# A group normalisation kernel: 24 of 32 tiles moved into a staggered loop, and GpSimd's share of the scaling moved to VectorE

## The chip, the cores and the metric

The kernel runs on one core of one Trainium2 chip. The time is device microseconds of that core. Two numbers are compared by the ratio of fast runs with its 95% interval, and "same" means within 2%.

## The reference

```python
def reference(x, g, b):            # x: bf16 (128, 1024, 32, 16), G = 32 groups
    xr = x.reshape(B, G, C // G, H, W)
    mu = xr.mean(axis=(2, 3, 4), keepdims=True)
    var = ((xr - mu) ** 2).mean(axis=(2, 3, 4), keepdims=True)
    xn = ((xr - mu) / jnp.sqrt(var + 1e-5)).reshape(B, C, H, W)
    return xn * g[None, :, None, None] + b[None, :, None, None]
```

Four images with 32 groups each fill 128 partitions, so there are 32 tiles of 128 x 16384 bf16, 4.19 MB each. A tile is loaded, summed, squared with the mean taken off, scaled channel by channel (32 channels of 512 elements) in place, and stored from the same buffer. There are six buffers.

## The kernel before

Per tile `i`: TensorE sums the tile into PSUM (`M`: 32 products with an identity matrix), VectorE reduces that to the mean (`R0`), ScalarE squares and sums the two halves (`Q`), then takes the root (`V`), and the 32 channels are scaled on three engines: 16 on VectorE, 13 on GpSimd (`A`), and the last 3 on ScalarE, between the two squares of the next tile (`finish`). `finish` also stores the tile and loads another into the buffer of an older one. SyncE issues these loads and stores in order. (PSUM is the memory in which the kernel keeps the sums of TensorE.)

```python
def Q(i):
    ...
    squares(st, F // 2, 0, st["negmean"][:], 1.0, s0[:])
    v0 = spool.tile([P, 1], F32, name="v0")
    finish(i - 1)                       # 3 channels on ScalarE, store i-1, load i+4
    ...                                 # v0 = s0 / n + eps, on GpSimd
    squares(st, F // 2, 1, st["negmean"][:], 1.0, s1[:])

def A(i):
    if not in_parts(i):
        for n in range(POOL_SHARE):                       # 13
            scale_on("pool", i, KC - LAST_SHARE - POOL_SHARE + n)
        for k in range(KC - LAST_SHARE - POOL_SHARE):     # 16
            scale_on("dve", i, k)
        ...

for i in range(NT):                     # 32 tiles, written out
    Q(i)
    if i + 1 < NT:
        M(i + 1)
        R0(i + 1)
    V(i)
    A(i)
```

## Time and profile before

| | before |
|---|---|
| time | 634.7 us |
| span of the profiled run | 631.9 us |
| DMA rate in the middle slices | 424 to 438 GB/s |
| ScalarE busy | 539 us (85%) |
| VectorE busy | 380 us (60%) |
| GpSimd busy | 347 us (55%) |

These are lines of the page of the kernel before. In all views PE is TensorE, PEld its weight load, DVE is VectorE, ACT is ScalarE, POOL is GpSimd and SPq is the queue of SyncE. The span is cut into 40 equal slices. A digit is the busy share of a slice in tenths (9 is 90% or more), and the last row is what the DMA engines moved.

```profile
ACT  4589999999999897877997779977989797797960
...
DMA  8999999999999999999999999999999999999996
GB/s 365 431 437 423 430 431 429 431 433 431 424 430 432 431 431 429 430 433 438 428 432 429 433 431 429 430 430 433 434 431 431 430 430 432 433 426 436 433 418 271
```

The DMA engines are full from the first slice to the last. The kernel moves 268.4 MB; at 430 GB/s that is 624 us. A tile costs them 8.39 MB / 430 GB/s = 19.5 us, in and out.

The next lines are the costliest groups of instructions of the kernel before: source line, engine, operation, tiles, shapes, count; then busy time in us and mean ns of one; then the idle time of the engine before them and what ended it.

```profile
L244 ACT ACTIVATE ja<-xt,negmean 128x8192 fp8e5<-128x8192 bf16 x60 | 426.7, 7112 | 52.1 <-DVE jd L189 52.0
...
L368 DVE TENSOR_SCALAR xt<-xt,scl,bia 128x512 bf16<-128x512 bf16 x536 | 352.6, 732 | 40.0 <-POOL bia L353 40.0
L368 POOL TENSOR_SCALAR xt<-xt,scl,bia 128x512 bf16<-128x512 bf16 x390 | 308.7, 806 | 3.4 <-POOL bia L353 0.3
```

ScalarE's two squares a tile are the largest compute cost. (The mean of a VectorE channel, 732 ns, counts overlap with its neighbours: 16 in a row take 11.14 us, 0.70 each.) ScalarE's work on one tile is in this timeline of the kernel before (start, us, what; in brackets the idle time before it and what ended it):

```profile
318.37 7.12 ACT L244 ACTIVATE ja<-xt,negmean 128x8192 fp8e5<-128x8192 bf16 x1 [1.43 <-DVE jd L189]
...
325.49 2.21 ACT L363 ACTIVATE xt<-xt,bia,scl 128x512 bf16<-128x512 bf16 x3
327.60 7.11 ACT L244 ACTIVATE ja<-xt,negmean 128x8192 fp8e5<-128x8192 bf16 x1
...
334.90 0.29 ACT L308 ACTIVATE rstd<-s,v 128x1 f32<-128x1 f32 x1
338.27 7.12 ACT L244 ACTIVATE ja<-xt,negmean 128x8192 fp8e5<-128x8192 bf16 x1 [3.08 <-DVE jd L189]
```

From 318.37 to 335.2 it works 16.8 us without a gap, then it waits for the next tile's mean, which waits for that tile's load.

The last view of the kernel before is the issuing queue's own waits on SyncE (us in total, times, longest), and the transfers with their median time from issue to landing:

```profile
SPq L101 <- DMA out_dram<-xt: 425.4, 26, 19.0
SPq L381 <- DVE xt L368: 151.7, 18, 38.6
```

```profile
xt<-in_x_dram SPq DMA_DIRECT2D x30, 4096.0 KB, 29.3
out_dram<-xt SPq DMA_DIRECT2D x30, 4096.0 KB, 38.3
```

SyncE waits mostly before issuing a load, for an older store to free its buffer. A store needs some 9.75 us of DMA time (half of a tile's 19.5) but lands 38 us after issue, so I estimate that three other transfers are queued ahead of it. Compute is well ahead of the queue.

### The profile page before, as it was taken

The page shows a single profiled execution, that of the slowest core. Times are in us where ns is not written, and L with a number is a line of the kernel's source. Part 1 is how long each engine was busy: PE and PEld are TensorE (multiplying, and loading weights), DVE is VectorE, ACT ScalarE, POOL GpSimd, SP SyncE. Part 2 cuts the span into 40 slices and gives each one's busy share as a digit, 9 for nine tenths or more (in the row PEclk, how much of TensorE's full clock was granted, in tenths as well). Part 3 has the DMA queues.
Part 4 walks back from the last instruction along what each step waited for, and adds up shares of the span by engine and source line. Part 5 has one row for each costly group of instructions (what it writes and reads, how often), then busy time and mean ns, then how long its engine had stood idle before and what let it go on. Part 6 is the DMA issues. An engine that isn't in the chain of part 4 may idle for free.

```text
span 631.9 us, 3907 instructions
## 1 busy us (share of the span) xinstructions
PE 293.1 (46%) x1025; PEld 114.4 (18%) x1025; DVE 380.2 (60%) x645; ACT 539.0 (85%) x268; POOL 346.8 (55%) x523
## 2 busy tenths in 40 slices
PE   5578604553245633456433565335553345647000
PEld 2233201221112211122111222112221112213000
DVE  1087666666676576545775457754657654577660
ACT  4589999999999897877997779977989797797960
POOL 0077666666666576544775446764557654477100
PEclk9689758766787657876678766677865788658655
DMA  8999999999999999999999999999999999999996
GB/s 365 431 437 423 430 431 429 431 433 431 424 430 432 431 431 429 430 433 438 428 432 429 433 431 429 430 430 433 434 431 431 430 430 432 433 426 436 433 418 271
DMA packets 11063, 268.70 MB, mean 425 GB/s; under 512 B 1312, under 2 KB 1312, under 8 KB 1312
## 3 DMA queue, kind: packets, MB, share of 16 engines
q1 hardware_dynamic: 10944, 268.44, 99.0%
q8 instruction: 8, 0.13, 0.1%
q14 instruction: 15, 0.12, 0.0%
q10 hardware_dynamic: 96, 0.00, 0.0%
HBM read 134.22 MB, written 134.22 MB: 425 GB/s over the span
## 4 chain that ended last, share of the span: by engine, by line
DMA 67%; ACT 15%; PE 7%; issue 4%; DVE 3%; POOL 0%; SPq 0%; DVEq 0%; ACTq 0%; POOLq 0%
DMA out_dram<-xt 42%; DMA xt<-in_x_dram 25%; ACT ja L244 13%; PE pa L166 7%; DVE xt L368 3%; ACT xt L363 2%; DMA gb_b<-in_g_dram 1%; POOL scl L337 0%; SPq L101 0%; ACT rstd L308 0%; DVE rstd L312 0%; DVE jd L189 0%; POOL shift L343 0%; DVEq L455 0%; DVE bia L324 0%
## 5 line engine op out<-in xcount | busy, mean ns | idle before, releaser
L244 ACT ACTIVATE ja<-xt,negmean 128x8192 fp8e5<-128x8192 bf16 x60 | 426.7, 7112 | 52.1 <-DVE jd L189 52.0
L166 PE MATMUL pa<-xt,eye 128*128 128x512 bf16 x976 | 281.8, 460 | 289.7 <-DMA xt<-in_x_dram 278.5
L368 DVE TENSOR_SCALAR xt<-xt,scl,bia 128x512 bf16<-128x512 bf16 x536 | 352.6, 732 | 40.0 <-POOL bia L353 40.0
L368 POOL TENSOR_SCALAR xt<-xt,scl,bia 128x512 bf16<-128x512 bf16 x390 | 308.7, 806 | 3.4 <-POOL bia L353 0.3
L166 PEld LDWEIGHTS <-eye 128*128 128x128 bf16 x1024 | 114.3, 114 | 468.5 <-DMA xt<-in_x_dram 290.6
L337 POOL TENSOR_SCALAR scl<-gb,rstd 128x32 f32<-128x32 f32 x31 | 11.2, 361 | 218.2 <-DVE rstd L312 218.2
L189 DVE TENSOR_SCALAR_CACHE_REDUCE jd<-pa 128x512 bf16<-128x512 f32 x32 | 22.0, 688 | 149.0 <-PE pa L166 149.0
L363 ACT ACTIVATE xt<-xt,bia,scl 128x512 bf16<-128x512 bf16 x98 | 72.0, 798 | 0.8 <-DVE bia L324 0.8
L244 ACT ACTIVATE ja<-xt,q 128x4096 fp8e5<-128x4096 bf16 x8 | 29.6, 3706 | 6.6 <-DVE jd L189 6.4
L312 DVE RECIPROCAL rstd<-rstd 128x1 f32<-128x1 f32 x32 | 5.1, 160 | 35.8 <-ACT rstd L308 35.8
L343 POOL TENSOR_SCALAR shift<-scl,negmean 128x32 f32<-128x32 f32 x31 | 11.2, 360 | 3.1
L216 POOL TENSOR_SCALAR off<-negmean,q 128x1 f32<-128x1 f32 x2 | 0.9, 432 | 20.5 <-DVE jd L189 20.5
L166 PE MATMUL pb<-xt,eye 128*128 128x512 bf16 x48 | 11.6, 388 | 1.0 <-DMA xt<-in_x_dram 1.0
L308 ACT ACTIVATE rstd<-s,v 128x1 f32<-128x1 f32 x30 | 8.8, 294 | 2.8
L244 ACT ACTIVATION_READ_ACCUMULATOR ja<-xt,negmean 128x1 f32 x60 | 11.2, 187 | 0.0
L353 POOL TENSOR_TENSOR bia<-shift,gb 128x32 f32<-128x32 f32 x31 | 7.8, 252 | 2.6
L308 ACT ACTIVATE rstd<-var,eps_t 128x1 f32<-128x1 f32 x2 | 0.6, 295 | 9.2 <-DVE jv L292 9.2
L273 POOL TENSOR_SCALAR v<-s 128x1 f32<-128x1 f32 x30 | 5.8, 192 | 2.5
L156 DVE COPY gb<-gb_p 128x64 f32<-128x64 f32 x1 | 0.2, 224 | 5.6 <-PE gb_p L148 5.6
L116 ACT ACT_TABLE_LOAD x1 | 1.3, 1283 | 1.7 <-PEq L444 1.7
L189 DVE DVE_READ_ACCUMULATOR jd<-pa 128x1 f32 x32 | 2.6, 81 | 0.0
L292 DVE TENSOR_SCALAR_CACHE_REDUCE jv<-sq,seed 128x4 f32<-128x4 f32 x2 | 0.4, 216 | 2.7 <-ACT ja L244 2.7
(18 smaller groups left out, 6.1 us busy)
## 6 DMA issues: line engine op xcount, KB each, us to landing
xt<-in_x_dram SPq DMA_DIRECT2D x30, 4096.0 KB, 29.3
out_dram<-xt SPq DMA_DIRECT2D x30, 4096.0 KB, 38.3
xt<-in_x_dram SPq DMA_DIRECT2D x8, 1024.0 KB, 16.5
out_dram<-xt SPq DMA_DIRECT2D x8, 1024.0 KB, 17.8
gb_b<-in_g_dram ACTq DMA_DIRECT2D x1, 2.0 KB, 3.2
gb_b<-in_b_dram ACTq DMA_DIRECT2D x1, 2.0 KB, 5.3
```

The source lines that it names most:

```text
L116: chain("act", nc.scalar.activation(out=warm[:], in_=eps_t[:], func=ACT.Sqrt))
L166: nc.tensor.matmul(out=ps[:], lhsT=eye[:], rhs=st["xt"][:, k * MMN : (k + 1) * MMN], start=(k == lo), stop=(k == hi - 1),),
L189: nc.vector.tensor_scalar(out=jd[:], in0=ps[:], scalar1=-inv_n, scalar2=seed, op0=ALU.mult, op1=ALU.add, accum_out=total[:],),
L244: nc.scalar.activation(out=ja[:, 0:w], in_=st["xt"][:, k * w : (k + 1) * w], func=ACT.Square, bias=bias, scale=scale, accum_out=sq, satura ...
L273: nc.gpsimd.tensor_scalar(out=v0[:], in0=s0[:], scalar1=inv_n, scalar2=EPS, op0=ALU.mult, op1=ALU.add,),
L308: nc.scalar.activation(out=rstd[:], in_=last_sum[:], func=ACT.Sqrt, bias=bias[:], scale=scale),
L312: chain("dve", nc.vector.reciprocal(out=rstd[:], in_=rstd[:]))
L337: nc.gpsimd.tensor_scalar(out=scl[:], in0=gam, scalar1=rstd[:], scalar2=None, op0=ALU.mult),
L343: nc.gpsimd.tensor_scalar(out=shift[:], in0=scl[:], scalar1=st["negmean"][:], scalar2=None, op0=ALU.mult,),
L353: nc.gpsimd.tensor_tensor(out=bia[:], in0=shift[:], in1=bet, op=ALU.add),
L363: inst = nc.scalar.activation(out=span, in_=span, func=ACT.Identity, bias=bia, scale=scl)
L368: inst = eng.tensor_scalar(out=span, in0=span, scalar1=scl, scalar2=bia, op0=ALU.mult, op1=ALU.add,)
```

## The change

The intent, as I read it: tiles 2 to 25 run in a loop of four trips of six tiles. One call of `tick` works on one tile, so a trip, one pass through the loop's body, is six ticks. The loop's head is aligned in memory for all engines (`head_align_engines`), I take it for the sake of instruction fetch. TensorE sums only half of a tile, and VectorE adds the two quarters of the other half in one instruction with an accumulator (`R`). GpSimd's 13 channels go to VectorE, which scales 29. The loop is "staggered": its body is cut into four stages, and the semaphores of a stage are reset while another runs. For that no engine may enter a stage before every engine has signalled that it is done with the stage two before. By default an engine gives this signal at the end of the stage in between, so a boundary is in effect a meeting of all five engines' instruction streams.

```diff
+    def M(s):
+        matmuls(s, banks[s], 0, NMM // 2)
+
+    def R(s):
+        t = small[s]
+        chain("dve", nc.vector.scalar_tensor_tensor(
+                out=jd[:], in0=xts[s][:, HF : HF + QF], scalar=1.0,
+                in1=xts[s][:, HF + QF : F], op0=ALU.mult, op1=ALU.add,
+                accum_out=t["half"][:], saturate=False))
+        sum_of(banks[s], 1.0, t["half"][:], t["total"][:])
+        ...
+    def A(s):
+        for k in range(KC - ACT_SHARE):          # 29
+            scale_on("dve", s, k)
+
+    def tick(i, s, load, cut):
+        before, after, free = (s - 1) % SLOTS, (s + 1) % SLOTS, (s - 2) % SLOTS
+        Q0(s)                                    # first square
+        finish(i - 1, before)                    # 3 channels on ScalarE, store i-1
+        if cut:
+            tc.stage_boundary()
+        if load:
+            L(i - 2 + SLOTS, free)
+        Q1(s)                                    # second square, root
+        M(after)
+        R(after)
+        V(s)
+        A(s)
 ...
+    with tc.For_i(
+        0, TRIPS * SLOTS, SLOTS, iteration_sync="staggered", hint_engines=(), head_align_engines=ENGINES
+    ) as iv:
+        for c in range(SLOTS):
+            tick(iv + FIRST + c, (FIRST + c) % SLOTS, True, c == 1 or c == 4)
+            if c == 2:
+                tc.stage_boundary()
+    last.clear()
+    tc.epilogue_barrier()
 ...
```

Two of the four boundaries lie behind `finish` in the middle of a tick (`c` = 1 and 4), two at the end of a tick (`c` = 2 and the loop's end). Also changed: the first load comes in halves, not quarters, the last load whole, and the last two stores in halves.

## The prediction

> **What bounds the kernel now.** The DMA engines. The table of 40 slices shows them at 90% or more in all slices but the first and last, at 424 to 438 GB/s; 268.4 MB at the usual 430 GB/s is 624 us of a 631.9 us span. In 4 us windows, data moves from about 2 us to 626 us without a gap. The Trainium skill (DMA: Bandwidth & Descriptors, Specifications) gives 435 GB/s as the fabric's ceiling; the trace agrees, at 430. So a tile (4.19 MB in, 4.19 MB out) takes 19.5 us. The other engines need less per tile: ScalarE two squares of 7.3 us, three channels (2.2 us) and a root, 17.1 us; VectorE 12 us (16 channels of 0.70 us, a 0.69 us sum); GpSimd 11.3 us; TensorE 9 to 10 us. The queue's own waits confirm it: before issuing loads it waits 425 us for earlier stores, so compute is ahead. A store takes 38 us to land and a load 29 us, four and three tiles' worth of one-way traffic: the queue is always deep.
>
> **What the change does, per tile.** GpSimd loses its 13 channels. VectorE takes 29, each at 0.33 us rather than 0.70 (the tile scaled without GpSimd near the end: 16 in 5.26 us), so 9.6 us; the skill (SBUF — State Buffer, Who interferes with whom) explains it: both engines share a port pair under an exclusive lock. VectorE also adds half of the tile: 4096 pairs, by the slope of the 0.69 us sum of 512 an estimated 4.3 us. VectorE: about 15 us, still under 19.5. TensorE sums 16 pieces, not 32: about 4.6 us, beside VectorE's half, so the mean comes some 4 us earlier. ScalarE is unchanged at 17.1 us. None of this is on the critical path, which is DMA.
>
> **What the loop adds.** Four stage boundaries a trip, at which engines wait for each other, and four trips. ScalarE now runs one to two tiles ahead of the DMA queue; the boundaries take some of this lead. I estimate delays up to 20 us for ScalarE at a boundary, and stores up to 10 us later, against 19.5 us or more of queued traffic: the DMA engines should not run dry inside the loop. Where they may: entering the loop (waiting for all six loads, landing at about 64 us, and the first store, at about 74 us, delays the second store: 0 to 4 us lost) and leaving it (a barrier that waits for the last loads and stores empties the queue; then a square of 7.3 us and three channels stand before the next store: 0 to 14 us). The end gains little: the last stores are queued behind older ones until 626 us, so a mean 4 us earlier is hidden. Fewer instructions save nothing visible: instruction fetches are 0.25 MB.
>
> **Prediction.** 635.5 us, 8 in 10 between 628 and 650. Faster by over 2% would need under 622 us, below the DMA time at 430 GB/s: 3%. Within 2%: 80%. Slower: 17%.
>
> **What would show it.** Right: 427 to 433 GB/s in all middle slices; VectorE channels at 0.33 us; GpSimd busy under 10%; TensorE about half; ScalarE still about 540 us. The two doubtful slices are at 60 to 80 us and near 520 us: a dip of GB/s there is the loop's entry or exit.
>
> **What would make it wrong.** An exit barrier that drains everything, or boundaries that stall the queue's issuing by more than 19.5 us every trip, would give 650 us or more. The half-tile add much above 4.3 us (over 9) would make VectorE the bound. A DMA rate that rises by a per cent[...], would give 628.

## More of the kernel before

A run is quoted as the median of its executions. The runs were taken on several chips; the kernel before was run again beside each, and its medians lie between 634.1 and 634.7 us.

## The result, and the profile after

| | before | after |
|---|---|---|
| time | 634.65 us (634.36 to 634.85, 4 runs) | 660.13 us (659.54 to 660.86, 4 runs) |
| span of the profiled run | 631.9 us | 659.1 us |
| ScalarE busy | 539 us | 539 us |
| VectorE busy | 380 us | 470 us |
| GpSimd busy | 347 us | 46 us |
| TensorE busy | 293 us | 166 us |

The ratio is 1.0402 (1.0384 to 1.042). A ratio is the mean time of one kernel's fast runs over that of the other's of the same rounds, so it is not quite the ratio of the medians quoted. The change is 25.5 us slower.

The same lines of the page, after:

```profile
ACT  3884987789598959877895989598778959999993
...
DMA  9999999999999999999999999999999999998576
GB/s 382 420 439 407 436 426 434 418 422 426 420 426 402 418 443 394 412 437 418 404 434 414 418 412 430 430 386 412 443 416 404 426 422 407 380 443 386 255 319 286
```

Two things changed. The middle slices no longer sit at 430: they swing around 418. And the last four slices, about 65 us, drop to 255 to 386, while ScalarE, nearly done with its work before, is now busy to the end. The windows of the changed kernel put numbers on both: three trips of the loop, and the end (the columns are the stretch, its length, busy us and instructions of PE, PEld, DVE, ACT and POOL, granted clock of TensorE, DMA share, GB/s).

```profile
106.00:226.80 120.80, 29.80 (x94) 11.06 (x96) 89.55 (x211) 100.25 (x49) 8.77 (x24) 0.61 1.00 420
226.80:347.50 120.70, 28.99 (x94) 10.93 (x96) 89.46 (x211) 100.14 (x49) 8.77 (x24) 0.63 0.99 419
347.50:468.20 120.70, 29.91 (x94) 11.21 (x96) 89.45 (x211) 100.01 (x49) 8.52 (x24) 0.61 0.99 418
...
600.00:648.00 48.00, 4.11 (x20) 1.67 (x17) 36.24 (x105) 46.16 (x30) 3.35 (x10) 0.60 0.67 284
```

A trip takes 120.7 us, 20.1 us a tile against 19.5; 24 tiles times 0.62 us are 15 us. The other 10 us are lost behind the loop: the rate is 401 GB/s from 542 to 580 us, and from 600 us on the DMA engines are busy two thirds of the time. There the last load, issued at 570.60, has landed (a load takes 24 us), and only stores are left. ScalarE finishes a tile in 16.8 us, and one store of 4.19 MB in 16.8 us is only 250 GB/s (an estimate from these two numbers). So a pace that is enough while loads and stores share the DMA engines is not enough at the end, unless stores are already waiting in the queue.

The DMA share in the trips still reads 0.99 to 1.00. The share of busy time alone would say "DMA bound"; the GB/s and the queue's waits say otherwise. In the changed kernel SyncE no longer waits for old stores before loading; it waits before storing, for compute. And its stores land after 15 us, not 38: the queue is shallow.

```profile
SPq L134 <- DVE xt L334: 408.5, 26, 33.8
SPq L134 <- ACT xt L330: 77.9, 9, 18.5
...
SPq L125 <- DMA out_dram<-xt: 4.9, 1, 4.9
```

```profile
xt<-in_x_dram SPq DMA_DIRECT2D x31, 4096.0 KB, 24.4
out_dram<-xt SPq DMA_DIRECT2D x30, 4096.0 KB, 15.0
```

The chain of work that ended last was DMA for 67% before (first line) and is ScalarE for 57% after (second line):

```profile
DMA 67%; ACT 15%; PE 7%; issue 4%; DVE 3%; POOL 0%; SPq 0%; DVEq 0%; ACTq 0%; POOLq 0%
ACT 57%; issue 21%; DVE 9%; DMA 7%; PE 3%; POOL 1%; ACTq 0%; SPq 0%; DVEq 0%; POOLq 0%
```

The groups that answer to those of before show that the pieces themselves cost what was forecast. The half-tile add, new, takes 4.42 us.

```profile
L254 ACT ACTIVATE ja<-xt,negmean 128x8192 fp8e5<-128x8192 bf16 x60 | 426.7, 7111 | 91.6 <-DVE xt L334 55.5
L334 DVE TENSOR_SCALAR xt<-xt,scl,bia 128x512 bf16<-128x512 bf16 x926 | 302.2, 406 | 40.7 <-POOL bia L320 40.6
...
L228 DVE SCALAR_TENSOR_TENSOR jd<-xt 128x4096 fp8e5<-128x4096 bf16 x30 | 132.6, 4419 | 12.2 <-issue 7.3
```

ScalarE's squares are as long as before, but ScalarE idles 91.6 us before them. Where it does is in its timeline over three ticks, half a trip:

```profile
239.72 7.12 ACT L254 ACTIVATE ja<-xt,negmean 128x8192 fp8e5<-128x8192 bf16 x1 [7.38 <-DVE xt L334]
...
263.56 2.21 ACT L330 ACTIVATE xt<-xt,bia,scl 128x512 bf16<-128x512 bf16 x3
268.35 7.12 ACT L254 ACTIVATE ja<-xt,negmean 128x8192 fp8e5<-128x8192 bf16 x1 [2.58 <-issue]
...
292.38 0.29 ACT L285 ACTIVATE rstd<-s,v 128x1 f32<-128x1 f32 x1
300.13 7.12 ACT L254 ACTIVATE ja<-xt,negmean 128x8192 fp8e5<-128x8192 bf16 x1 [7.46 <-DVE xt L334]
```

From 239.72 to 300.13 are 60.4 us for three tiles: 50.4 us of work without gaps, and 2.58 us at the mid-tick boundary and 7.46 us at the end-of-tick boundary. Three tiles of DMA are 58.5 us. So in the loop ScalarE with its two waits is slower than the DMA engines, by 1.9 us per three tiles. Eight such pairs of waits, and 11.05 us once at the loop's entry, make up the 91.6 us.

Whom does it wait for? These are VectorE's channels and SyncE's issues of the same stretch:

```profile
258.03 9.47 DVE L334 TENSOR_SCALAR xt<-xt,scl,bia 128x512 bf16<-128x512 bf16 x29 [1.29 <-POOL bia L320]
...
294.15 9.46 DVE L334 TENSOR_SCALAR xt<-xt,scl,bia 128x512 bf16<-128x512 bf16 x29 [1.29 <-POOL bia L320]
```

```profile
267.70 0.34 SPq L134 DMA_DIRECT2D out_dram<-xt  x1
268.65 0.35 SPq L125 DMA_DIRECT2D xt<-in_x_dram  x1
```

At the end of a tick ScalarE has delivered the root at 292.67. VectorE scales its 29 channels from 294.15 to 303.6, and its signal stands behind them. ScalarE goes on at 300.13, some 3.5 us before the last channel ends: my reading, which no run tests, is that VectorE's instruction stream runs some ten short instructions ahead of its arithmetic (in e3 below the gap is 3.6 us, with 32 channels). At the mid-tick boundary the one who is late is SyncE: its store (267.70) waits for VectorE's channels (done at 267.5), and ScalarE goes on at 268.35. So ScalarE waits for VectorE, whose channels in turn waited for ScalarE's root. In the written-out kernel ScalarE starts the next square in this time.

### The profile page after: what moved, and what is told of

It reads as the page before. It is cut to its first block, busy times and chain, and to the rows that moved or that the text cites. A ratio compares the mean times of both kernels' runs of the same rounds, so it can differ in the third digit from the quotient of the medians.

```text
span 659.1 us, 3426 instructions
## 1 busy us (share of the span) xinstructions
PE 166.1 (25%) x535; PEld 62.7 (10%) x545; DVE 470.1 (71%) x1126; ACT 538.8 (82%) x268; POOL 45.7 (7%) x133
## 4 chain that ended last, share of the span: by engine, by line
ACT 57%; issue 21%; DVE 9%; DMA 7%; PE 3%; POOL 1%; ACTq 0%; SPq 0%; DVEq 0%; POOLq 0%
ACT ja L254 48%; DVE xt L334 8%; ACT xt L330 8%; DMA out_dram<-xt 4%; DMA xt<-in_x_dram 3%; PE ps L195 3%; ACT rstd L285 1%; POOL scl L300 0%; POOL shift L310 0%; POOL bia L320 0%; DVE jd L207 0%; DVE rstd L296 0%; SPq L125 0%; DVE sp_jv L398 0%; ACTq L450 0%
## 5 line engine op out<-in xcount | busy, mean ns | idle before, releaser
L254 ACT ACTIVATE ja<-xt,negmean 128x8192 fp8e5<-128x8192 bf16 x60 | 426.7, 7111 | 91.6 <-DVE xt L334 55.5
L334 DVE TENSOR_SCALAR xt<-xt,scl,bia 128x512 bf16<-128x512 bf16 x926 | 302.2, 406 | 40.7 <-POOL bia L320 40.6
L195 PE MATMUL ps<-xt,eye 128*128 128x512 bf16 x518 | 159.3, 476 | 414.8 <-issue 288.3
L228 DVE SCALAR_TENSOR_TENSOR jd<-xt 128x4096 fp8e5<-128x4096 bf16 x30 | 132.6, 4419 | 12.2 <-issue 7.3
L195 PEld LDWEIGHTS <-eye 128*128 128x128 bf16 x544 | 62.6, 118 | 540.5 <-issue 483.4
L207 DVE TENSOR_SCALAR_CACHE_REDUCE jd<-ps,half 128x512 fp8e5<-128x512 f32 x30 | 22.5, 751 | 14.9 <-PE ps L195 12.4
L254 ACT ACTIVATE ja<-xt,sp_q 128x4096 fp8e5<-128x4096 bf16 x8 | 29.7, 3708 | 2.8 <-DVE jd L207 2.5
L270 POOL TENSOR_SCALAR v<-s 128x1 f32<-128x1 f32 x30 | 13.1, 436 | 244.5 <-ACT ja L254 244.5
L195 PE MATMUL bank_a<-xt,eye 128*128 128x512 bf16 x16 | 7.1, 628 | 23.2 <-DMA xt<-in_x_dram 23.2
L207 DVE TENSOR_SCALAR_CACHE_REDUCE jd<-bank_a 128x512 fp8e5<-128x512 f32 x2 | 1.4, 686 | 6.6 <-PE bank_a L195 6.6
L242 DVE TENSOR_SCALAR negmean<-total 128x1 f32<-128x1 f32 x30 | 4.6, 154 | 1.0
```

Source lines behind the costliest of these rows:

```text
L195: nc.tensor.matmul(out=ps[:], lhsT=eye[:], rhs=xts[s][:, k * MMN : (k + 1) * MMN], start=(k == lo), stop=(k == hi - 1),),
L207: nc.vector.tensor_scalar(out=jd[:, 0:MMN], in0=ps[:], scalar1=factor, scalar2=seed, op0=ALU.mult, op1=ALU.add, accum_out=total, saturate= ...
L228: nc.vector.scalar_tensor_tensor(out=jd[:], in0=xts[s][:, HF : HF + QF], scalar=1.0, in1=xts[s][:, HF + QF : F], op0=ALU.mult, op1=ALU.add ...
L254: nc.scalar.activation(out=ja[:, 0:w], in_=xts[s][:, k * w : (k + 1) * w], func=ACT.Square, bias=bias, scale=scale, accum_out=sq, saturate ...
L270: nc.gpsimd.tensor_scalar(out=t["v0"][:], in0=t["s0"][:], scalar1=inv_n, scalar2=EPS, op0=ALU.mult, op1=ALU.add,),
L334: inst = nc.vector.tensor_scalar(out=span, in0=span, scalar1=scl, scalar2=bia, op0=ALU.mult, op1=ALU.add,)
```

## The experiments

The theory: the stage boundaries make ScalarE and VectorE take turns; 20 us of waits a trip exceed ScalarE's slack of 6 x 2.7 = 16 us a trip; and since ScalarE never gets ahead of the queue, the tiles behind the loop run at ScalarE's pace. The rivals: the new split (29 channels and the half-tile add on VectorE) is slower by itself; or the back edge (the jump from the end of the loop's body to its head) and instruction fetch cost the time; or the loop's entry and exit do.

All outputs are right.

| run | time, us | ratio to before (95%) |
|---|---|---|
| e1 loop written out | 636.9 | 1.0044 (1.0031 to 1.0058) |
| e2 VectorE signals early | 645.1 | 1.0175 (1.016 to 1.0191) |
| e3 no channels on ScalarE | 662.2 | 1.0443 (1.0427 to 1.0459) |
| e4 two trips | 642.6 | 1.0131 (1.0115 to 1.0146) |
| e5 e2 and two trips | 636.5 | 1.0031 (1.0016 to 1.0046) |
| e6 e1, no channels on ScalarE | 637.2 | 1.0047 (1.0032 to 1.0062) |
| e7 no half-tile add | 685.5 | 1.0811 (1.0795 to 1.0828) |
| e8 e1, last parts in quarters | 636.7 | 1.0045 (1.0031 to 1.0059) |
| e9 all engines signal early | 634.6 | 1.0001 (0.9986 to 1.0016) |
| e10 not aligned | 660.2 | 1.04 (1.0384 to 1.0416) |
| e11 e8, first load in quarters | 637.2 | 1.0046 (1.0032 to 1.006) |
| e12 before, GpSimd's channels to VectorE | 636.1 | 1.0027 (1.0014 to 1.0041) |
| e13 e9 with three trips | 634.0 | 0.999 (0.9977 to 1.0004) |
| e14 e9, one channel on ScalarE | 633.3 | 0.9978 (0.9965 to 0.9992) |

**e1: the loop written out.**

```diff
-    tc.prologue_barrier()
-    with tc.For_i(0, TRIPS * SLOTS, SLOTS, iteration_sync="staggered", ...) as iv:
-        for c in range(SLOTS):
-            tick(iv + FIRST + c, (FIRST + c) % SLOTS, True, c == 1 or c == 4)
-            if c == 2:
-                tc.stage_boundary()
-    tc.epilogue_barrier()
+    for i in range(FIRST, FIRST + TRIPS * SLOTS):
+        tick(i, i % SLOTS, True, False)
```

> The changed kernel with the loop written out: the same ticks in the same order, the same split of the work, no stage boundaries. Theory (boundaries): ScalarE works 16.8 us a tile and loses 10.0 us per three tiles at the boundaries, 60.4 us against 58.5 us of DMA; without boundaries it needs 50.4 us, DMA is the bound again, and the kernel takes 632 to 637 us, with ScalarE idle in no fixed pattern and stores landing 35 us or more after issue. Rival (the new split: 29 channels and the half-tile add on VectorE): the time stays above 652 us.

Measured: 636.9 us. The whole split of the work is kept, and 23 of the 25.5 us are gone, so the split by itself is not the cause. The queue is deep again; stores land 38 us after issue. The issuing queue's waits of this run are as before:

```profile
SPq L125 <- DMA out_dram<-xt: 462.3, 26, 19.5
SPq L134 <- DVE xt L333: 116.9, 11, 32.7
```

**e2: only VectorE's signal moved to an early place in each stage.**

```diff
         M(after)
         R(after)
+        if early:                       # ticks 0, 1, 3 and 4: once in each stage
+            tc.previous_stage_wait(mybir.EngineType.DVE)
         V(s)
         A(s)
```

> The changed kernel with its loop; only VectorE's signal that its previous stage is done stands early in each stage (after the mean of the next tile), not behind the 29 channels at the end of the stage. Theory: the 7.4 us that ScalarE idles at every other boundary is the wait for VectorE's sequencer to get through those channels; it falls to 2 us or less, the loop falls from 60.4 to 58.5 to 59 us per three tiles, and the kernel takes 635 to 645 us. Rivals (the back edge and its instruction fetch, or the new split): 657 to 662 us.

Measured: 645.13 us, just above the range. Nothing but the place of a signal was changed, and it is worth 15 us. ScalarE's timeline in this run shows the end-of-tick wait at 1.50 us rather than 7.46, with the mid-tick wait now 3.94 to 6.84 us (2.57 only at the first boundary):

```profile
286.12 7.12 ACT L256 ACTIVATE ja<-xt,negmean 128x8192 fp8e5<-128x8192 bf16 x1 [1.50 <-issue]
...
318.53 7.12 ACT L256 ACTIVATE ja<-xt,negmean 128x8192 fp8e5<-128x8192 bf16 x1 [3.94 <-issue]
```

From 227.33 to 286.12 to 344.27, three tiles take 58.8 and 58.2 us: the loop runs at the DMA's pace. What is left, 8 us against e1, lies at the end (columns as in the windows above):

```profile
560.00:580.00 20.00, 5.70 (x16) 2.08 (x17) 16.89 (x43) 19.92 (x9) 2.32 (x7) 0.67 0.99 415
580.00:600.00 20.00, 8.99 (x32) 3.47 (x31) 18.17 (x47) 19.91 (x9) 1.34 (x4) 0.76 0.86 369
600.00:612.00 12.00, 0.00 (x0) 0.00 (x0) 5.51 (x18) 11.79 (x9) 1.34 (x4) 0.50 0.62 265
```

ScalarE is busy all the time there, and from 580 us on the DMA engines are not: compute left the loop without a lead.

**e3: no channels on ScalarE, 32 on VectorE.** Edit: `ACT_SHARE = 3` becomes `0`, which holds for all tiles but the last two, inside the loop and outside.

> The changed kernel with no channels on ScalarE in the loop: VectorE takes all 32. Theory (ScalarE's work and the boundary idle add up): ScalarE per three tiles 44 us of work, idle 8.4 and some 5.7 us at the two boundaries, since VectorE's channels take 1 us longer, sum 58 us, so near the DMA's 58.5; the end is shorter too; 635 to 645 us. Rival (VectorE has too much work): slower than the changed kernel, above 662 us.

Measured: 662.2 us, where my theory said 635 to 645. This is a miss. I had treated the waits as sums with fixed parts. The mid-tick wait was as forecast (5.6 us), but the one at the end of a tick grew to 10.9 us, not 8.4:

```profile
302.43 7.12 ACT L254 ACTIVATE ja<-xt,negmean 128x8192 fp8e5<-128x8192 bf16 x1 [10.94 <-DVE xt L334]
...
329.96 7.12 ACT L254 ACTIVATE ja<-xt,negmean 128x8192 fp8e5<-128x8192 bf16 x1 [5.58 <-issue]
```

In that tick VectorE takes the reciprocal at 354.87, behind its own mean work for the next tile, although ScalarE had the root at 352.3. With less to do, ScalarE only waits longer; three tiles take 60.7 us, about as in the changed kernel. It is a chain of turns, not a sum on one engine. By its time alone this run fits the rival "VectorE has too much work" as well, so e6 was made.

**e4: two trips, twelve tiles written out behind them.** Edit: `TRIPS = 4` becomes `2`.

> Two trips of the loop rather than four; 12 tiles are written out behind it. Theory: each looped tile costs the DMA engines 0.6 us, and 12 are enough for 7 us; behind the loop ScalarE catches up at 17 us a tile against 19.5, so the end is bound by DMA as in the kernel before: 640 to 646 us. If the cost were at the loop's entry and exit rather than inside, it would stay at 657 to 662 us.

Measured: 642.6 us, as forecast. Half the looped tiles cost 5.7 us over e1. In the 36 us behind the loop the rate is 403 GB/s, which costs an estimated 2 us against 430; after that it is back at 421 to 441 GB/s in every slice but the last. Entry and exit, which are both still there, are not where most of the time goes.

**e5: e2 and e4 together.**

> VectorE's early signal and two trips together. Theory: with the early signal the loop runs at the DMA's pace (58.0 to 58.7 us per three tiles), and what was left of the loss, 8 us, came from ScalarE leaving the loop without a lead over the queue; twelve tiles written out behind the loop give the lead back, so the end is bound by DMA: 636 to 639.5 us, as the kernel with the loop written out (636.9). Rival (entering the loop or the new split costs the rest): 642 us or more.

Measured: 636.5 us, as e1, though entry and exit of the loop are still there. Its loop runs at the DMA's pace and its written-out tiles win the lead back; together these return everything that writing the loop out returns.

**e6: e1 with all 32 channels on VectorE.** Edit: e1 and `ACT_SHARE = 0`.

> All 32 channels on VectorE, and the loop written out. The looped kernel with this split took 662.2 us. Theory (there the boundaries make ScalarE and VectorE take turns; VectorE's load by itself, some 16.5 us a tile against 19.5 of DMA, is harmless): 635 to 639 us. Rival (VectorE with 32 channels is too slow whatever the loop): above 650 us.

Measured: 637.2 us. The split that took 662.2 us in the loop is harmless without it. This settles e3: at these loads VectorE matters only through the boundaries.

**e7: no half-tile add; TensorE sums all 32 pieces.**

```diff
-        matmuls(s, banks[s], 0, NMM // 2)
+        matmuls(s, banks[s], 0, NMM)
-        chain("dve", nc.vector.scalar_tensor_tensor(...))       # the half-tile add
-        sum_of(banks[s], 1.0, t["half"][:], t["total"][:])
+        sum_of(banks[s], 1.0, None, t["total"][:])
```

> The changed kernel with its loop, but TensorE sums all 32 pieces and VectorE adds no half. Theory (a chain through the boundaries: behind the mid-tick boundary ScalarE's second square, 7.3 us, used to hide the sum for the next tile; 32 products at the low clock and the reduction take about 11 us): some 3 to 4 us more per three tiles, so 680 to 695 us. Rival (the half-tile add on VectorE is what slows the change): below 650 us.

Measured: 685.5 us. The half-tile add is not the cause; in this loop it helps. Behind the mid-tick boundary a third wait appears, for the mean of the next tile. It is some 3.06 us in one half of a trip and 2.05 in the other:

```profile
289.80 7.12 ACT L241 ACTIVATE ja<-xt,negmean 128x8192 fp8e5<-128x8192 bf16 x1 [3.06 <-DVE negmean L229]
...
352.42 7.12 ACT L241 ACTIVATE ja<-xt,negmean 128x8192 fp8e5<-128x8192 bf16 x1 [2.05 <-DVE rstd L283]
```

That is a little less than the 3 to 4 us I had written. Three tiles take 63.65 us (250.43 to 314.08) and 62.6 us (314.08 to 376.69) in turn, against 60.4. From ScalarE's first tile in the loop to its first one behind it are 505.3 us, against 483.6 in the changed kernel: 22 of the 25 us added. The other 3 were lost before the loop, which ScalarE enters at 61.79 us and not at 58.69.

**e8 and e11: the written-out kernel with the last load and stores in quarters (e8), and the first load in quarters too (e11), as in the kernel before.** Edits: the last load gets four parts; the last two tiles are stored after every eight channels; in e11 `2 if i == 0` becomes `NQ if i == 0`.

> The loop written out, and the last load and the last two stores in quarters as in the kernel before, not in one piece and in halves. Written out in halves it was 0.44% slower than before. Theory: bytes end at the same time in both, and the rest is the coarser last stores (16 KB rather than 8 KB pieces, so one engine finishes late): 633.5 to 635 us. If the residue lies elsewhere: 636 to 637.5 us.

> The loop written out, the last load and stores in quarters, and the first load in quarters too, as before. It looks for the 0.4% that is left against the kernel before. If the coarse first load is the cause: 633.5 to 635 us; if not, 636 to 637.5 us.

Measured: 636.7 and 637.2 us. Both guesses at the last 0.4% were wrong: neither changes the time, so the size of the first and last transfers is not it.

**e9: all engines signal early.**

```diff
             L(i - 2 + SLOTS, free)
+        if early and not cut:
+            tc.previous_stage_wait(mybir.EngineType.SP)
         Q1(s)
         M(after)
         R(after)
+        if early:
+            for e in (DVE, PE, Activation, Pool):
+                tc.previous_stage_wait(e)
```

> Four trips, and every engine's signal early in the stage: VectorE, TensorE, ScalarE and GpSimd after the mean of the next tile, and in every other stage SyncE after its first load. With VectorE's alone it took 645.1 us, and ScalarE still idled 4 to 7 us at the boundary in the middle of a tick, at which SyncE comes late because its store waits for VectorE's channels and then the queue. Theory: that idle falls in the loop's stages, ScalarE keeps some lead over the queue at the exit: 636 to 643 us. If the other engines' signals don't matter: 644 to 646 us.

Measured: 634.6 us, ratio 1.0001. This is better than the 636 to 643 us of my theory, which is a miss in its size. The loop, the alignment, the split and the boundaries are all kept, and the whole 25.5 us are gone. The waits did not all shrink: the end-of-tick wait reads 6.2 to 6.3 us, the mid-tick one 1.9. But three tiles take 58.5 us, and ScalarE waits for SyncE, which waits for the DMA queue; it is slack now, not a turn. The first two lines are ScalarE's timeline, the last is SyncE's largest wait in total, which in the changed kernel was for VectorE's channels (408.5 us).

```profile
280.36 7.12 ACT L256 ACTIVATE ja<-xt,negmean 128x8192 fp8e5<-128x8192 bf16 x1 [6.30 <-DVE xt L336]
...
338.83 7.12 ACT L256 ACTIVATE ja<-xt,negmean 128x8192 fp8e5<-128x8192 bf16 x1 [6.19 <-DVE xt L336]
...
SPq L136 <- DMA out_dram<-xt: 237.8, 22, 18.1
```

The releaser is given as VectorE's channels, though VectorE signals before them; SyncE's next load, issued at 279.55 and 338.10, is what stands just before both starts. This run moves the signals of four more engines than e2 at once; which of them matters was not tried one by one.

**e10: without the alignment to a fetch block.** Edit: `head_align_engines=ENGINES` removed.

> The changed kernel without the alignment of the loop to a fetch block. Theory: at the back edge ScalarE idles 7.4 us, as at the boundary in the middle of the body, so in the aligned kernel fetching costs nothing that shows; unaligned it may cost a few us at three back edges: 658 to 680 us. If alignment itself were what slows the change: below 655 us.

Measured: 660.2 us, the same as with it, and the waits are the same (7.37 and 2.57 us). Neither the alignment nor its absence costs anything that shows here. The two end-of-tick boundaries are equally long (7.38 and 7.46 us), though only the second of them has a back edge.

**e12: the kernel before, with GpSimd's channels on VectorE.** Edit: `POOL_SHARE = 13` becomes `0`.

> The kernel before with one part of the change: GpSimd's 13 channels go to VectorE, nothing else. Theory: no compute engine is the bound there, VectorE's channels fall from 0.70 to 0.33 us each and take 9.6 us a tile rather than 11.2: 633.5 to 635.5 us. If the new split is what costs the 0.4% left over: 636 to 637.5 us.

Measured: 636.1 us, ratio 1.0027. The theory's range is missed by 0.6 us, and the other forecast's is met: this part alone brings more than half of the 0.4%. Yet e9, which has it too, does not show the 0.4%, so it is no fixed price of the split.

**e13 and e14: e9 with three trips, and e9 with one channel on ScalarE and 31 on VectorE.**

> All signals early and three trips. Theory (lead at the exit): six tiles written out behind the loop win back six times 2.4 us, so 425 GB/s or more up to 620 us, and the last bytes land 3 to 6 us earlier than with four trips: 629 to 633 us. Rival (a deep queue lets single DMA engines fall behind, so that one engine is still moving bytes long after the mean of them): 634 to 637.5 us, with a thin rest of 10 to 100 GB/s over the last 8 us, as in the kernels with the loop written out.

> All signals early, four trips, one channel on ScalarE and 31 on VectorE. Theory (lead at the exit): ScalarE needs 15.6 us a tile rather than 17.1, so the tiles behind the loop end some 8 us earlier and the DMA engines do not run dry: 627 to 633 us. If VectorE's two channels more bring the boundary's wait back: 640 us or more. Rival (single DMA engines falling behind): 634 to 637.5 us.

Measured: 634.0 us and 633.3 us. In e13 the theory's rate came true and its time did not. These are the windows of its last stretch:

```profile
616.00:620.00 4.00, 0.00 (x0) 0.00 (x0) 0.00 (x0) 0.00 (x0) 0.00 (x0) 0.50 0.99 426
620.00:624.00 4.00, 0.00 (x0) 0.00 (x0) 0.00 (x0) 0.00 (x0) 0.00 (x0) 0.50 0.86 369
624.00:628.00 4.00, 0.00 (x0) 0.00 (x0) 0.00 (x0) 0.00 (x0) 0.00 (x0) 0.50 0.25 107
628.00:632.00 4.00, 0.00 (x0) 0.00 (x0) 0.00 (x0) 0.00 (x0) 0.00 (x0) 0.50 0.06 25
```

The rate holds to 620 us, then a thin rest runs for eight more: a share of 0.06 equals one of 16 engines still at work. e1 has the same rest, with shares of 0.21, 0.06 and 0.01 in 624 to 636 us, and so has the kernel before, with 0.49 and 0.09 in 624 to 632 us. In e9, whose queue is shallow at the end, the rate falls earlier but the engines end together (1.02, then 0.83 in its last two stretches). So my reading is that a lead at the exit is worth a few us, and that a deep queue gives about as much back by ending unevenly.

The windows also suggest where the 0.3 to 0.5% of e1, e5, e6, e8, e11 and e12 lies: in this rest. At 624 us e1 has about 0.48 MB left to move and the kernel before about 0.98 MB, so e1 is ahead; but nothing moves after 631 us in the kernel before, and in those six bytes still move after 632 us (one profiled run of each). Why the engines end so unevenly stays open.

e14 falls between its two forecasts (627 to 633 us, and 634 to 637.5). It is the fastest kernel: 0.22% below before, which is clear of noise but no gain to speak of; the bound is still DMA.

## Why the prediction was wrong

1. **The bound of the kernel before: right.** DMA, at 430 GB/s. The Trainium skill gives 435 GB/s as the fabric's ceiling (DMA: Bandwidth & Descriptors, Specifications). The means over long stretches stay below it, at 430 GB/s from 0 to 600 us in the kernel before, in e1 and in e9; single slices read up to 448 (e11). No kernel here beat the 624 us of DMA time. e1, with everything but the loop, came out at 636.9, inside the range.
2. **The costs of the pieces: right.** A VectorE channel without GpSimd took 9.46 / 29 = 0.33 us, and the half-tile add 4.42 us (4.3 forecast). The skill's exclusive lock on the port pair (SBUF — State Buffer, Who interferes with whom) agrees: 0.70 us with GpSimd at work (16 channels in 11.14 us in the timeline of before), 0.33 without. GpSimd fell to 7%; ScalarE stayed at 539 us.
3. **"The DMA engines should not run dry inside the loop": this step failed.** The boundaries themselves were not underrated: I allowed up to 20 us for ScalarE at one, and none in the loop took more than 7.5 after the entry. What was wrong is what I compared them with. I set one delay (up to 10 us for a store) against the queue's depth (19.5 us). Depth absorbs a delay once. A delay that returns has to be set against the slack of the engine that suffers it: 19.5 - 16.8 = 2.7 us a tile, 16 us a trip, of which the prediction's own 17.1 would leave 14. The boundaries took 20 us a trip (two times 2.6 and 7.4). The prediction named a stall of 19.5 us a trip as the danger limit, for the queue's issuing; it should have summed the waits of ScalarE. The deficit, 3.7 us a trip, used up the lead, and from then on ScalarE set the pace: 15 us in all (e2 gives them back).
4. **"So a mean 4 us earlier is hidden", and the end stays as it was: wrong for the same reason.** It assumed that compute still leads at the end. Compute left the loop with no lead, and the last stores came at ScalarE's pace of one in 16.8 us: some 10 us, the exit in point 5 included (e9 is 10.5 us faster than e2, which had lost only this; e5, which is e2 with two trips, gives back 8.7).
5. **Entry and exit: within the forecast, and not the cause.** At the entry ScalarE waited 11.05 us, but no DMA time was lost: over the first 106 us the mean rate is 419 GB/s, and 420 in the kernel before and in e1, which has no loop. At the exit ScalarE's wait was 7.96 us, like any end-of-tick boundary; the 38 us behind it ran at 401 GB/s, an estimated 2.6 us lost against 430 (0 to 14 forecast). e5 has both and takes the time of e1.
6. **"Fewer instructions save nothing visible": right** as far as the runs go (e9, with the loop, takes the time of the kernel before), and e10 adds that the alignment is worth nothing visible either.

What is shown: the time is lost through the place of the stage signals (e2 and e9 change nothing else), the more the more tiles are looped (e4: 5.7 us over e1 with 12 tiles, against 23.2 with 24), and not through the split by itself (e1, e6), the add (e7) or the alignment (e10). The back edge is still there in e9, which loses nothing. What is argued only: that VectorE's instruction stream passes the boundary ahead of its last channels. What stays open: which of the signals of e9 are needed, and why the last transfers end unevenly in the kernels that are 0.3 to 0.5% slower than before.

## What to carry to other kernels

Before putting a software pipeline into a loop with synchronised stages, list for each boundary who arrives last and on whom that engine had been waiting; if A waits for B and B has just waited for A, the overlap of the two is gone there. Compare the sum of such waits over a trip with the slack of the busiest compute engine over the same trip, not with the depth of a queue. A signal placed as soon as the older work is done, rather than at the stage's end, can cost nothing, and here it returned all 25 us; and a DMA share near 1 does not prove a DMA bound, where the issuing queue waits for compute and stores land early.

## What the Trainium skill lacked or had wrong

- No page tells of loops with staggered semaphore resets. A boundary cost ScalarE 7.4 us where VectorE signals behind 29 channels of 0.33 us, and 1.5 us where it signals before them.
- VectorE: DVE Perf Modes, the perf-mode tier table, has no row for an add of two tensors with scalar and accumulator: 128x4096 bf16 from SBUF took 4.42 us, or 1.08 ns for each of the 4096 pairs.
- DMA: Bandwidth & Descriptors, Where 436 GB/s comes from, says that for HBM to SBUF transfers the HBM side (about 358 GB/s) binds. With this one core at work it did not: 430 GB/s, half in and half out, for 600 us. So the sentence holds too widely; the page's own note that its higher numbers are single-core numbers fits.
- The same page does not say how evenly the 16 engines end behind a deep queue: in e13 a share of 0.25 and then 0.06 went on for 8 us after the rate had left 369 GB/s.
- Runtime: NRT & Kernel Launch, Instruction fetch mechanics, warns of a fetch stall at a taken branch whose target is not in the window. This is not refuted, but no run here shows such a stall: 660.17 us unaligned, 660.13 us aligned, and a wait of 7.46 us at the back edge against 7.38 at the boundary without one. Whether the target had left the window was not looked at.
